# Clearing the block diagonal earlier, and GpSimd's local attention on 256 columns

## The chip, the cores and the metric

The kernel runs on one core of a Trainium2 chip. The core's engines run side by side, each through its own instruction list in order: TensorE (PE in the profile, PEld for its weight loads), VectorE (DVE), ScalarE (ACT), GpSimd (POOL) and SyncE (SP, which issues most DMAs). GpSimd issues some DMAs as well. The metric is device time in microseconds (us) of one execution.

## The reference

Two attention blocks read the same x (2048 tokens, 512 columns, 32 heads of 16) and are mixed by a gate of one number a token:

```python
x = A_x
g = _sigmoid((x * gate_w).sum(-1, keepdims=True))
a = _A_ref(x, A_wqkv, A_wo)   # full softmax attention, 32 heads of 16
b = _B_ref(x, B_wqkv, B_wo)   # each token attends to 8 keys: pos - 0, 2, 4, ... 14
return g * a + (1 - g) * b
```

```python
# _B_ref, the local dilated attention
off = jnp.arange(W) * dil                      # W, dil = 8, 2
idx = pos[:, None] - off[None, :]
logits = jnp.einsum("bhsd,bhswd->bhsw", q, kg) * scale     # kg, vg: k, v at idx
logits = jnp.where(mask[None, None, :, :], logits, -1e9)
attn = _softmax(logits, axis=-1)
o = jnp.einsum("bhsw,bhswd->bhsd", attn, vg)
```

## The kernel before

**Block A** is the bulk. It runs through 32 periods, one for each chunk of 512 queries (4) and group of four heads (8). In a period, PE forms scores of 128 keys by 512 queries for a head (32 x 128 weights from `kt_all`, `qt` streaming) into PSUM tiles (`ring`), ACT takes the exponential of two or three such tiles at a time into `pT`, and PE multiplies `pT` by the values (`vp_all`) into an accumulator. For 3 to 12 tiles a period, the exponential is made on DVE instead (`d_set`, line 1294): a TENSOR_SCALAR from PSUM writes a uint16 number whose bits are a rough exponential, and two more TENSOR_SCALARs within SBUF (`raise1` and `raise2`, lines 1336 and 1339, on 1536 and 3072 columns of `pd_a` or `wall`) add constants to it, so that four weighted copies (`vd_all`) can be summed by PE. These two are called shifts below.

**Block B** is laid beside it. Per chunk of queries and per 8 heads, `scores_of` projects keys into `kt_b` and queries into `qb`; SP copies `qb` head by head into a block-diagonal tile `q_bd` (line 983), which must be zero elsewhere; PE multiplies blocks of the two, DVE copies the result to `sev`, and it goes through DRAM so that each query has its 8 logits in a row. `b_tile` (line 1050) then handles 128 tokens: softmax of `lg` (DVE, GpSimd, ACT), eight products of gathered value rows with attention weights on GpSimd (`av_mul`, line 1109: four into `av`, four into two tiles `prod`), sums of the halves, and a last sum `av_last` (line 1151) into `obb`, which PE transposes (`fin`, line 1190). For 14 of the 16 tiles the sums before the last are DMAs that GpSimd issues and that accumulate into `av` (`av_sum`); for the last two tiles they are GpSimd additions (`av_add`). `HB` (line 923) is the number of columns that one GpSimd product or addition works on; it is `D`, 512.

**The start.** x and the weights of A are loaded; PE transposes x; `k3` (line 619) and `q2` (line 626) rearrange key and query weights for PE's tiles, in part on DVE and in part on GpSimd. `o_q2` (line 635) holds the two halves of q2: group 0 on DVE, group 1 on GpSimd. `init_bd` (line 606) clears `kt_b` and `q_bd`; the first key projections of block B on DVE (`ke`) and the SP copies into `q_bd` wait for it.

**What sets the order.** Every step is an `Op` with an engine, a planned length, a due time and dependencies. `list_schedule` (line 182) simulates the engines with these lengths and always takes the ready step that is due first; `rel` holds a step back in the plan until a time. The result is one order for all, and `chain_on` (line 351) makes each engine keep it. The plan's times don't exist at run time: an engine runs its list as soon as semaphores allow. `GP` (line 111) gives the planned length of a GpSimd step: 0.14 us plus a part proportional to the columns, in which the plan lets no SBUF-to-SBUF work of DVE run (`port`). Calls go through a wrapper, so L371 stands for all instructions of DVE, ACT, GpSimd and SP, and L380 for matmuls.

Of the kernel before, what the change touches and what calls it, by code (L numbers as in the profile page):

```python
# [31 lines left out]
DH = 16  # L32
NG = 8
W = 8
# [14 lines left out]
ROWB = 2 * NGR * QW  # L49
SPREAD = (0.75, 0.88, 0.6)  # L50
STEP = 32.0
ZB = 27.0
WEIGHTS = (0.83984375, 0.70703125, 0.59375)


def _ap(base, dims):
    return bass.AP(tensor=base.tensor, offset=base.offset, ap=[list(d) for d in dims])
# [53 lines left out]
GP = lambda kind, n: [(False, PRE), (True, NS[kind] * n)]  # L111
# [197 lines left out]
def kernel(  # L309
# [15 lines left out]
    S, D = x2d.shape  # L325
# [3 lines left out]
    DC = D // 128  # L329
# [46 lines left out]
    G = Chained(nc.gpsimd, "pool")  # L376
# [20 lines left out]
    def op(eng, occ, fn, dl, **kw):  # L397
        if any(tk.kind == "misc" for tk in kw.get("use", ())):
            dl -= URG[eng]
        o = Op(eng, occ, fn, dl, **kw)  # L400
        ops.append(o)
        return o
# [3 lines left out]
    def tok(tag, cap):  # L406
        name = "banks" if tag in ("misc", "acc") else tag
        if name not in res:
            res[name] = Banks(3) if name == "banks" else Res(cap)
        return Tok(res[name], tag)  # L410
# [15 lines left out]
    for pi in range(NP):  # L426
        first_unit.append(nu)
        n = n_dve[pi]
# [14 lines left out]
    for pi, (own, groups) in enumerate(seq):  # L443
        n = sum(len(g) for g in groups)
# [26 lines left out]
    w0 = DC * 2 * D  # L471
# [39 lines left out]
    q_bd = const.tile([128, 8, QW], BF16, name="q_bd")  # L511
    kt_b = const.tile([128, 2, 2, W - 1 + QW // 2 + 9], BF16, name="kt_b")
# [40 lines left out]
    o_init_p = op("pool", 2.8, init_pool2, -8.0, deps=[o_perm])  # L553
# [49 lines left out]
    o_wq = op("sp", 0.5, load_w(0), -8.5, lat=12.5)  # L603
    o_wv = op("sp", 0.5, load_w(2), -8.4, lat=13.0)
    o_bw = op("sp", 1.0, load_bw, -8.3, lat=19.0)
    def init_bd(n):
        def s():
            if n == 0:
                G.memset(kt_b[:], 0.0)
            G.memset(q_bd[:, 2 * n:2 * n + 2], 0.0)  # L610
        return s
    o_zb = o_init_p
    for n in range(4):
        o_zb = op("pool", 1.0 + 0.5 * (n == 0), init_bd(n), 27.0 + n, deps=[o_zb], rel=ZB)
    o_zr = op("sp", 0.6, load_zero, -8.2, deps=[o_wz], use=[zt], lat=19.0)
    o_wo = op("sp", 5.5, load_wo, WO, rel=WO, lat=10.0)

# [1 line left out]
    def k3(E, i0, i1):  # L619
        def s():  # L620
            wk = wkw.rearrange("p c (i j d) -> p c i j d", i=NG, j=4)
            for e, j in ((0, 3), (1, 0)):
                E.tensor_copy(out=wk3[:, :, i0:i1, e, :], in_=wk[:, :, i0:i1, j, :])
        return s

    def q2(E, i):
        def s():
            a0 = wq[:, :, 4 * i * DH:4 * (i + 1) * DH]
            for e in range(2):
                E.tensor_copy(out=wq2[:, :, 4 * i:4 * i + 4, e, :], in_=a0.rearrange("p c (j d) -> p c j d", j=4))  # L630
        return s

    o_k3 = [op("dve", 0.2, k3(V, 0, 1), -4.0, deps=[o_wk])]
    o_k3 += [op("pool", 2.0, k3(G, 1, NG), -3.0, deps=[o_wk, o_init_p])] * (NG - 1)
    o_q2 = [op("dve", 0.5, q2(V, 0), 0.0, deps=[o_wq]), op("pool", 1.5, q2(G, 1), 5.0, deps=[o_wq, o_k3[1]])]

    def warm():
# [6 lines left out]
    for sc in range(NC):  # L644
        st = {}
# [253 lines left out]
    for sc in range(NC):  # L899
        a = op("pe", 0.9, zmm(sc), GT + sc, full=1, deps=[o_bw, a] + o_xt[sc], alloc=[tzp] if sc == 0 else [],  # L900
               use=[tzp] if sc else [], rel=20.0)
# [18 lines left out]
    o_kvd, o_obt = [], []  # L920
    obt_tiles, obt_tok = {}, {}
    WP = WH // 2
    HB = D
    o_lgw = {}

    def v_rows(t):
# [123 lines left out]
    def b_tile(t):  # L1050

        st = {}
        tb = BT[t]
        cb, e, hb = t // TPC, t // 2 % 2, t % 2
        tvs = [tok("gat", NGA), tok("gat", NGA)]
        tlg, tbb = tok("lg", 2), tok("obb", 1)
# [49 lines left out]

        hn = HB // DH

        def av_mul(hf, wp, w_, c0):
            def s():  # L1110
                if hf == 0:
                    o_ = av[:, wp + w_, c0:c0 + HB]
                else:
                    if w_ == 0 and c0 == 0:
                        st["av", wp] = work.tile([128, WP, D], FP32, name="prod", tag="prod", bufs=NPR)
                    o_ = st["av", wp][:, w_, c0:c0 + HB]
                attn = st["lg"]
                w0 = hf * WH + wp + w_
                a0 = attn[:, 0, w0, 0:1]
                attn_bc = _ap(a0, [list(a0.ap[0]), [8 * W, DC], [1, 8], [0, DH]])  # L1120
                G.tensor_tensor(out=o_.rearrange("p (c h d) -> p c h d", c=DC, d=DH),
                                in0=st["vsh", hf][:, wp + w_, :].rearrange("p (c h d) -> p c h d", c=DC, d=DH),
                                in1=attn_bc, op=ALU.mult)
            return s

# [8 lines left out]
        def av_add(wp, w_, c0):  # L1134
            def s():
                cs = slice(c0, c0 + HB)
                d_, a_ = (wp or 0) + w_, av[:, WP + w_, cs] if wp is None else st["av", wp][:, w_, cs]
                G.tensor_tensor(out=av[:, d_, cs], in0=av[:, d_, cs], in1=a_, op=ALU.add)
            return s

        def sums_of(wp, deps, use):

            if t < NT - 2:
                return op("pool", DMAQ, av_sum(wp), tb + 5, deps=deps, use=use, lat=DMAQ + DMAL, far=True, name=f"B{t}")
            a_ = None
            for w_ in range(WP):
                for c0 in range(0, D, HB):
                    a_ = op("pool", 0.0, av_add(wp, w_, c0), tb + 5, deps=deps, after=[a_], use=use, name=f"B{t}", parts=GP("ff", HB))
            return a_

        def av_last(c0):
            def s():
                if c0 == 0:
                    st["obb"] = work.tile([128, D], BF16, name="obb", tag="obb", bufs=1)
                G.tensor_tensor(out=st["obb"][:, c0:c0 + HB], in0=av[:, 0, c0:c0 + HB], in1=av[:, 1, c0:c0 + HB], op=ALU.add)
            return s
# [14 lines left out]
        tav = tok("av", 1)  # L1171
        b, sums = None, []
        for hf, wp in halves:
            tp_ = tok("prod", NPR) if hf else None
            for n_, (w_, c0) in enumerate((w_, c0) for w_ in range(WP) for c0 in range(0, D, HB)):
# [3 lines left out]
                       name=f"B{t}", parts=GP("bf", HB))  # L1179
# [1 line left out]
                b = sums_of(wp, [b], [tav, tp_])  # L1181
                sums.append(b)
        a1 = sums_of(None, sums, [tav])
        a1 = op("pool", 0.0, av_last(0), tb + 6, deps=[a1], alloc=[tbb], use=[tav], name=f"B{t}", parts=GP("ff", HB))
        a1.lat += SM_LAT[3]
        tk = tok("misc", 2)
        if cb not in obt_tok:
# [16 lines left out]
    for cb in range(NC):  # L1204
        for t in range(TPC * cb, TPC * (cb + 1)):
            v_rows(t)
        for c in range(DC):
            scores_of(cb, c)
        for t in range(TPC * cb, TPC * (cb + 1)):
            b_tile(t)  # L1210
# [157 lines left out]
    for k, us in enumerate(sets):  # L1368
        ring = "rA" if k % 2 == 0 else "rB"
        n = len(us)  # L1370
# [4 lines left out]
        st = dict(k=k, us=us, tn=tn, tp=tp)  # L1375
# [7 lines left out]
        def ex(st=st, n=n, k=k):  # L1383
# [5 lines left out]
               alloc=[tr_], use=[q_tok[pi] for pi in pis], after=[last_qk[0]], scores=k % 2, name=f"qk{k}")  # L1389
# [15 lines left out]
    for pi, (c_, i) in enumerate(periods):  # L1405
        st = {}
# [43 lines left out]
        if i % 2 == 0:  # L1450
# [4 lines left out]
                       use=[to] + ([oat_tok[c_]] if i > 1 else []))  # L1455
# [5 lines left out]
    for t in range(NT):  # L1461
        c_, tt = t // TPC, t % TPC
        st = {}
# [30 lines left out]
        for k0 in range(0, DC + nh, 2):  # L1494
            nk = min(2, DC + nh - k0)
            a = op("pe", WAVE(nk), ab_part(k0), dl - 2.0 + 0.3 * k0, full=nk,
                   deps=[a] if k0 else [o_oat[NG * c_ + ng - 1], o_wo] + o_obt[TPC * c_:TPC * (c_ + 1)],
                   alloc=[tk] if k0 == 0 else [], use=([tk] if k0 else []) + [oat_tok[c_], obt_tok[c_]])
# [67 lines left out]
```

## Time and profile before

| | |
|---|---|
| three runs | 839.07, 845.14, 848.81 us; median 845.14 |
| profiled execution | 837.14 us, span 835.3 us |
| granted TensorE clock in it | 0.991 |
| first exponential of block A starts, last one ends | 23.04 us, 824.4 us |
| GpSimd products `av<-vsh,lg` and `prod<-vsh,lg` | 64 of 1203 ns and 64 of 1250 ns (mean) |
| GpSimd last sums `obb<-av` | 16 of 1447 ns (mean) |
| DVE shifts, `pd_a`: 3072 and 1536 columns | 65 of 1115 ns and 65 of 705 ns (mean) |
| DVE shifts, `wall`: 3072 and 1536 columns | 48 of 1174 ns and 48 of 690 ns (mean) |

How to read the lines: a group has the engine, the operation, tile written <- tiles read, the shape, how many (x); then busy us and the mean in ns of one, then idle time of that engine just before them and what ended it. In a timeline the columns are the start in us from the span's start, the duration, the engine, and in brackets the idle time before and what ended it; where it says x2, neighbours are merged into one line and the duration is that of both. The chain of waits is followed back from the last instruction, and each line of it has a start and a duration. The time of an execution is its span and a little around it (1.84 us here).

### The profile page before, as it was taken

Reading aid. Unit: us, or ns where it says so; the run is one execution under the profiler, and the core shown is the slowest. Engines: PE = TensorE matmul, PEld = TensorE weight load, DVE = VectorE, ACT = ScalarE, POOL = GpSimd, SP = SyncE. Lnnn points to the kernel's source line nnn. Section 1 sums busy time; section 2 is a strip of 40 time slices with the busy share of each in tenths; the row PEclk is TensorE's granted clock in tenths of the full one; section 3 lists DMA queues with packets and bytes.
Section 4 is the critical chain, followed back from the end, with each engine's and each line's share of the span. In section 5 each row is a group of like instructions: output and inputs, shape, how many; then the busy total and the mean of one; then the engine's idle time right before and its main releaser. Section 6 shows DMA issues by size and latency. Waiting matters only on the chain.

```text
span 835.3 us, 18731 instructions
## 1 busy us (share of the span) xinstructions
PE 754.8 (90%) x7426; PEld 249.3 (30%) x7483; DVE 627.8 (75%) x1023; ACT 789.1 (94%) x706; POOL 308.7 (37%) x358
## 2 busy tenths in 40 slices
PE   7999899999989999889889998998999989998996
PEld 4433333333222222222222222222323222222221
DVE  5644866887766779988987777777987687788756
ACT  2899898999999999999999999999999989999994
POOL 5000000545662161654611513434530166394700
PEclk9999999999999999999999999999999989999998
DMA  7301115167447362527362260716153453620000
GB/s 253 78 2 46 42 38 125 39 122 136 122 127 186 51 122 50 131 44 190 76 162 39 68 110 1 155 15 163 32 116 103 78 109 76 121 64 1 1 2 25
DMA packets 118103, 71.44 MB, mean 86 GB/s; under 512 B 76272, under 2 KB 109056, under 8 KB 118016
## 3 DMA queue, kind: packets, MB, share of 16 engines
q1 hardware_dynamic: 111968, 48.23, 22.3%
q0 software_dynamic: 6048, 22.02, 14.6%
q8 instruction: 58, 0.95, 0.5%
q14 instruction: 29, 0.24, 0.1%
HBM read 29.11 MB, written 17.00 MB: 55 GB/s over the span
## 4 chain that ended last, share of the span: by engine, by line
ACT 35%; PE 33%; issue 15%; DVE 11%; DMA 3%; SPq 3%; ACTq 0%; DVEq 0%; POOL 0%
ACT pT L371 35%; PE misc_ps L380 22%; PE ring L380 10%; DVE pd_a L371 4%; DVE wall L371 4%; SPq L371 3%; DMA lg<-lg_scr 1%; DMA xld<-in_A_x_dram 1%; DMA lg_scr<-sev 1%; DMA q_bd<-qb 0%; DMA q_scr<-qa 0%; DVE qb L371 0%; DVE vp_all L371 0%; PE pxt L653 0%; DVE osb L371 0%
## 5 line engine op out<-in xcount | busy, mean ns | idle before, releaser
L371 ACT ACTIVATE pT<-ring 128x1536 bf16<-128x1536 f32 (+1 forms) x684 | 781.2, 1293 | 26.5 <-PE ring L380 17.1
L380 PE MATMUL ring<-qt,kt_all 32*128 32x512 bf16 x1709 | 271.0, 384 | 47.0 <-ACT pT L371 40.1
L380 PE MATMUL misc_ps<-pT,vp_all 128*17 128x512 bf16 (+1 forms) x1709 | 217.1, 385 | 1.2 <-DVE qb L371 0.5
L380 PEld LDWEIGHTS <-kt_all 32*128 32x128 bf16 x2048 | 84.2, 91 | 288.1 <-issue 278.0
L371 DVE TENSOR_SCALAR pd_a<-misc_ps 128x512 uint16<-128x512 f32 x195 | 131.8, 683 | 49.8 <-PE misc_ps L380 46.0
L380 PE MATMUL misc_ps<-qt,kt_all 32*128 32x512 bf16 x339 | 125.7, 382 | 2.6 <-DVE pd_a L371 0.9
L371 DVE TENSOR_SCALAR pd_a<-pd_a 128x1536 uint16<-128x1536 uint16 (+1 forms) x130 | 117.8, 910 | 9.5 <-PE misc_ps L380 8.6
L380 PE MATMUL misc_ps<-z 128*32 128x512 bf16 x374 | 121.9, 388 | 1.6 <-DVE z L371 1.6
L371 DVE TENSOR_SCALAR wall<-misc_ps 128x512 uint16<-128x512 f32 x144 | 96.4, 684 | 25.6 <-PE misc_ps L380 23.4
L371 DVE TENSOR_SCALAR wall<-wall 128x1536 uint16<-128x1536 uint16 x96 | 89.0, 932 | 20.5 <-PE misc_ps L380 19.9
L380 PEld LDWEIGHTS <-vp_all 128*17 128x17 bf16 (+1 forms) x2048 | 59.0, 89 | 84.3 <-issue 66.9
L371 POOL TENSOR_TENSOR prod<-vsh,lg 128x512 f32<-128x512 bf16 x64 | 76.3, 1250 | 0.0
L371 POOL TENSOR_TENSOR av<-vsh,lg 128x512 f32<-128x512 bf16 x64 | 75.4, 1203 | 1.0
L380 PE MATMUL misc_ps<-pd_a,vd_all 128*17 128x512 bf16 x585 | 72.5, 383 | 1.6 <-DVE pd_a L371 1.1
L371 POOL TENSOR_TENSOR rden<-rden,g_rw 128x16 f32<-128x16 f32 x30 | 10.1, 338 | 160.7 <-DVE rden L371 160.6
L380 PE MATMUL misc_ps<-wall,vd_all 128*17 128x512 bf16 x432 | 53.8, 386 | 2.9 <-DVE wall L371 2.8
L380 PEld LDWEIGHTS <-vd_all 128*17 128x17 bf16 x1017 | 31.8, 89 | 60.1 <-issue 53.9
L380 PEld LDWEIGHTS <-z 128*32 128x32 bf16 x374 | 32.6, 96 | 41.4 <-issue 22.1
L380 PE MATMUL misc_ps<-xT,wall 128*32 128x512 bf16 x544 | 41.2, 387 | 3.0 <-DVE wall L371 2.3
L371 POOL TENSOR_SCALAR rr<-rr,omg 128x32 f32<-128x32 f32 x16 | 7.5, 470 | 86.0 <-DVE rr L371 61.6
L371 DVE TENSOR_SCALAR_CACHE_REDUCE kt_all<-misc_ps,rowc 128x512 bf16<-128x512 f32 x32 | 23.9, 749 | 19.7 <-PE misc_ps L380 19.3
L371 POOL TENSOR_TENSOR lg<-lg,mx 128x256 f32<-128x256 f32 x16 | 13.1, 816 | 69.2 <-DVE mx L371 69.2
(95 smaller groups left out, 645.3 us busy)
## 6 DMA issues: line engine op xcount, KB each, us to landing
vsh<-kv_scr SPq DMA_DIRECT2D x128, 128.0 KB
av<-prod POOLq DMA_DIRECT2D x28, 512.0 KB, 5.3
lg_scr<-sev SPq DMA_DIRECT2D x16, 540.0 KB
av<-av POOLq DMA_DIRECT2D x14, 512.0 KB, 5.4
qt<-q_scr SPq DMA_DIRECT2D x30, 128.0 KB
q_bd<-qb SPq DMA_DIRECT2D x128, 16.0 KB
kv_scr<-kvs SPq DMA_DIRECT2D x16, 128.0 KB
lg<-lg_scr SPq DMA_DIRECT2D x64, 32.0 KB
```

The lines of the kernel that those rows point to most:

```text
L371: return chain_on(key, f(*a, **k))
L380: return chain(nc.tensor.matmul(out, lhsT=lhsT, rhs=rhs, start=start, stop=stop, **kw))
```

## The change

The clears lose their release time (`ZB`, 27 in plan time) and their due times of 27 to 30; they follow GpSimd's key-weight copies (`o_k3[1]`) and are due at -2.0 to -1.7, ahead of GpSimd's query-weight copies, due at 5. `HB` becomes 256, so each product, each `av_add` and each last sum becomes two instructions of half the columns, with half-width access patterns of the weights and the value rows.

```diff
-ZB = 27.0
...
-    o_zb = o_init_p
-    for n in range(4):
-        o_zb = op("pool", 1.0 + 0.5 * (n == 0), init_bd(n), 27.0 + n, deps=[o_zb], rel=ZB)
...
     o_k3 = [op("dve", 0.2, k3(V, 0, 1), -4.0, deps=[o_wk])]
     o_k3 += [op("pool", 2.0, k3(G, 1, NG), -3.0, deps=[o_wk, o_init_p])] * (NG - 1)
     def init_bd(n):
         def s():
             if n == 0:
                 G.memset(kt_b[:], 0.0)
             G.memset(q_bd[:, 2 * n:2 * n + 2], 0.0)
         return s
+    o_zb = o_k3[1]
     for n in range(4):
+        o_zb = op("pool", 1.0 + 0.5 * (n == 0), init_bd(n), -2.0 + 0.1 * n, deps=[o_zb])
     o_q2 = [op("dve", 0.5, q2(V, 0), 0.0, deps=[o_wq]), op("pool", 1.5, q2(G, 1), 5.0, deps=[o_wq, o_k3[1]])]
...
-    HB = D
+    HB = D // 2
...
                 w0 = hf * WH + wp + w_
-                a0 = attn[:, 0, w0, 0:1]
-                attn_bc = _ap(a0, [list(a0.ap[0]), [8 * W, DC], [1, 8], [0, DH]])
-                G.tensor_tensor(out=o_.rearrange("p (c h d) -> p c h d", c=DC, d=DH),
-                                in0=st["vsh", hf][:, wp + w_, :].rearrange("p (c h d) -> p c h d", c=DC, d=DH),
+                a0 = attn[:, c0 // 128, w0, 0:1]
+                attn_bc = _ap(a0, [list(a0.ap[0]), [8 * W, HB // 128], [1, 8], [0, DH]])
+                G.tensor_tensor(out=o_.rearrange("p (c h d) -> p c h d", c=HB // 128, d=DH),
+                                in0=st["vsh", hf][:, wp + w_, c0:c0 + HB].rearrange("p (c h d) -> p c h d", c=HB // 128, d=DH),
                                 in1=attn_bc, op=ALU.mult)
...
-        a1 = op("pool", 0.0, av_last(0), tb + 6, deps=[a1], alloc=[tbb], use=[tav], name=f"B{t}", parts=GP("ff", HB))
+        for c0 in range(0, D, HB):
+            a1 = op("pool", 0.0, av_last(c0), tb + 6, deps=[a1], alloc=[] if c0 else [tbb], use=[tav] + ([tbb] if c0 else []),
+                    name=f"B{t}", parts=GP("ff", HB))
```

More of the change, by code (lines that the diff above doesn't have):

```diff
@@ L605 @@
     o_bw = op("sp", 1.0, load_bw, -8.3, lat=19.0)
[L606 to L611, printed above, removed]
-    o_zb = o_init_p
-    for n in range(4):
-        o_zb = op("pool", 1.0 + 0.5 * (n == 0), init_bd(n), 27.0 + n, deps=[o_zb], rel=ZB)
     o_zr = op("sp", 0.6, load_zero, -8.2, deps=[o_wz], use=[zt], lat=19.0)
@@ L634, with init_bd, s @@
     o_k3 += [op("pool", 2.0, k3(G, 1, NG), -3.0, deps=[o_wk, o_init_p])] * (NG - 1)
+    def init_bd(n):
+        def s():
+            if n == 0:
+                G.memset(kt_b[:], 0.0)
+            G.memset(q_bd[:, 2 * n:2 * n + 2], 0.0)
+        return s
+    o_zb = o_k3[1]
+    for n in range(4):
+        o_zb = op("pool", 1.0 + 0.5 * (n == 0), init_bd(n), -2.0 + 0.1 * n, deps=[o_zb])
     o_q2 = [op("dve", 0.5, q2(V, 0), 0.0, deps=[o_wq]), op("pool", 1.5, q2(G, 1), 5.0, deps=[o_wq, o_k3[1]])]
```

## The prediction

> **What bounds the kernel now.** I read the page first, then the waits of ACT, the first 26 us of the chain of waits, and the timelines of GpSimd, DVE and ACT at the places those pointed to. The page:
>
> ```profile
> PE 754.8 (90%) x7426; PEld 249.3 (30%) x7483; DVE 627.8 (75%) x1023; ACT 789.1 (94%) x706; POOL 308.7 (37%) x358
> L371 ACT ACTIVATE pT<-ring 128x1536 bf16<-128x1536 f32 (+1 forms) x684 | 781.2, 1293 | 26.5 <-PE ring L380 17.1
> ```
>
> ACT's 684 exponentials are 781.2 us of the span of 835.3. What is not ACT's own work is little: 23.04 us until the first exponential, 26.5 us of idle time before exponentials (8.9 of them already inside those 23), and about 11 us behind the last one, which ends at 824.4. So an edit pays only if it shortens the 23 us of the start, the 17.6 us that remain of the idle time, or the 11 us of the tail. GpSimd at 37% is no bound by its sum.
>
> The start, from the chain of waits, and what GpSimd and DVE do there:
>
> ```profile
> 13.57 0.69 DVE xT L371
> 14.26 3.34 DVE wall L371 x2
> 17.60 0.04 issue
> 17.64 3.58 PE misc_ps L380 x50
> ...
> 23.04 3.71 ACT pT L371 x3
> ```
>
> ```profile
> 6.58 1.07 POOL L371 COPY wall<-wall 128x448 bf16<-128x448 bf16 x2 [1.23 <-DMA wall<-in_A_wqkv_dram]
> 12.18 0.74 POOL L371 COPY wall<-wq 128x256 bf16<-128x256 bf16 x2 [4.54 <-DMA wq<-in_A_wqkv_dram]
> 12.87 1.01 POOL L371 MEMSET kt_b<- 128x1088 bf16 x1
> 13.81 3.64 POOL L371 MEMSET q_bd<- 128x1024 bf16 x4
> ```
>
> ```profile
> 14.18 3.41 DVE L371 COPY wall<-wq 128x256 bf16<-128x256 bf16 x2
> ```
>
> DVE's two copies of the first query weights (q2, into a part of `wall`) take 3.41 us, and they end at 17.59, just behind GpSimd's memsets (17.45). A copy of 512 columns within SBUF that meets no GpSimd work (the four fills of kt_all at 22.13 and 23.39) takes 0.41, so the rest is waiting for GpSimd. PE's first query projection, and with it the first exponential, stands behind these copies. And between 7.65 and 12.18 GpSimd is idle.
>
> The later idle time shows the same meeting. The worst place, DVE, GpSimd and ACT:
>
> ```profile
> 678.82 3.71 DVE L371 TENSOR_SCALAR wall<-wall 128x3072 uint16<-128x3072 uint16 x1 [1.33 <-PE misc_ps L380]
> ```
>
> ```profile
> 678.70 0.90 POOL L371 DMA_DIRECT2D av<-prod  x1 [0.30 <-POOL prod L371]
> 679.37 2.34 POOL L371 TENSOR_TENSOR prod<-vsh,lg 128x512 f32<-128x512 bf16 x2
> ```
>
> ```profile
> 684.04 2.37 ACT L371 ACTIVATE pT<-ring 128x1536 bf16<-128x1536 f32 x2 [1.02 <-PE ring L380]
> 687.48 3.80 ACT L371 ACTIVATE pT<-ring 128x1536 bf16<-128x1536 f32 x3 [1.07 <-PE misc_ps L380]
> ```
>
> This shift over 3072 columns takes 0.95 where GpSimd is idle (686.07). Here it outlasts a descriptor instruction and two products that stand behind it; ACT then idles 1.02 us, and 1.07 more one step later.
>
> **Part 1, the clears.** The five memsets (1.01 + 3.64, from 12.87 to 17.45 = 4.58 us) move ahead of GpSimd's q2 copies, right behind its key-weight copies. They would run from 7.6 to 12.2, in time that GpSimd now waits for a DMA; its own q2 copies start at 12.2 instead of 12.18. DVE has nothing from SBUF to SBUF in 7.65 to 12.2 (its rows there read PSUM, and such rows keep their 0.69 beside GpSimd work later), so the cover is whole. DVE's q2 copies then start at 14.18 with GpSimd idle. Their price is not in the trace unblocked: at least the 0.29 to 0.35 of the 256-word masks (qa, qt), at most the 0.41 of a 512-column fill, each; I take 0.35, nearest in size, so they end at 14.9 instead of 17.59 (2.7 earlier). What is late next: PE's key projection, until 15.37 instead of waiting to 17.64, which leaves 2.3 us to gain on PE; the two reductions behind it on DVE (17.51 and 18.18) move up 2.6. I take 2.4 us. Bounds: 2.7 above. Below, a loss: if DVE's own key-weight copy at 6.55 were caught by the memsets behind GpSimd's two copies, it would wait to 12.2; DVE's work from there to q2 sums to 4.4 us plus about 1 of PE, so q2 ends at about 18.3, 0.7 later than now. I don't expect it: that copy got its turn between GpSimd's two. The waits for the cleared tiles (DVE's kt_b cast, SP's q_bd stores) come first at about 60 us and hold nothing.
>
> **Part 2, 256 columns.** Costs on GpSimd: 16 columns take 0.22 (rden), 256 take 0.62 (ott), so 0.19 fixed and 1.67 ns a column, which gives 1.05 for 512, the products' own undisturbed time. A split therefore costs 0.19. Split are 128 products, 12 sums of the last two tiles and 16 last sums: 156 x 0.19 = 30 us more on GpSimd, 37% becomes 41%. Of one tile it is 8 + 1 splits, 1.7 us (the last two, with six sums, 2.9). What hides it: a tile's result (obb) is read late. The last obb ends at 787.99 and PE transposes it at 795.4; chunk 0's last user starts at 278. Without that cover it would be 2.9 at the end.
>
> Gains are in DVE's waits. The shifts' means by shape against 0.95 and 0.56 undisturbed: 65 x (1.115 - 0.95) + 48 x (1.174 - 0.95) + 65 x (0.705 - 0.56) + 48 x (0.690 - 0.56) = 37 us of waiting. Met singly, an instruction of 0.62 instead of 1.05 makes the mean wait 41% shorter. But ACT's idle time does not come from the single waits (at most 1.1 us, which the buffers absorb): the gaps that follow a port wait stand before 303.6 (0.53 us), 413.7 (0.66), 684.0 (1.02) and its echo at 687.5 (1.07), 3.3 us together, and each begins in two products whose spans overlap, as above: 2.34 us for two that last 1.3 each. In such a stretch DVE gets no turn between them, and four halves, 4 x 0.62 plus the same overlap, hold it just as long (2.5 to 2.8). So I take 0 for part 2, with bounds of 3.3 gained and 0.5 lost in this execution.
>
> The Trainium skill (SBUF — State Buffer, Who interferes with whom) has the pair of ports go to whoever starts first, for one whole instruction. By that rule the DVE shift of 678.82 would have had its turn after the first product, and with halves 41% of the 3.3 us, 1.4 us, would come back: 833.3 instead of 834.7 below. The trace speaks against it in these stretches (it waited through two) and for it elsewhere.
>
> **Re-planning.** The order of every engine is written out from planned costs, and those of the products change (0.14 + 0.91 planned for one, now twice 0.14 + 0.46). Up to the first product, at 156 us, I expect the order to stay; behind it PE, DVE and ACT instructions may change places. No row prices that; zero is the middle, and it is the widest of the unknowns.
>
> **Sum.** The profiled execution took 837.14 (835.3 span, 1.84 around it): minus 2.4 is 834.7. The three plain runs have a median of 845.14, 8.0 above it, and spread over 9.7 us, so about 1% is what a measurement of this kernel can tell from no change. Minus 2.4 on the median is **842.7**.
>
> **Rivals.**
> *Port waits matter more than this execution shows* (0.33). The plain runs are 8.0 us longer than the profiled one with the same order, so stalls differ from run to run; if they are port meetings, 8.0 + 3.3 = 11.3 us can go. For it: 66 of DVE's shifts and masks from SBUF to SBUF take over 60 ns more than undisturbed, and PE's order stands behind many. Against: ACT lost only 3.3 to them here. With 75% recovered, 845.1 - 2.4 - 8.5 = 834.2; it passes 1% from 6.1 us on.
> *The new order puts PE behind longer stretches* (0.27), slower. Between two accumulating DMAs GpSimd now has four overlapping instructions, and there are 28 such stretches (av<-prod x28). One shift that is caught there and that PE waits for costs ACT 1.02 + 1.07 = 2.1 us. In this execution that is fully so once; seven more make 14.7, less 2.4 gives 857.4. It decides from five or six (10.9 us) on. For it: idle ACT time behind 140 us is only some 9 us of the 17.6, so a different order has more to lose than to win. Against: buffers absorb most meetings.
> *The start's gain does not arrive* (0.04): the caught copy above, 0.7 later, 845.8.
>
> **How the numbers follow.** The forecast has 0.36. Within 1% (836.7 to 853.6): forecast and last rival, 0.40. Faster 0.33, slower 0.27, from the two others. The forecast's own range is 836 to 849: 3.3 + 0.3 better, 0.5 + 3.1 worse by the bounds, and 3 us of re-planning to each side. To leave out no more than 2 in 10 the range reaches past 834.2 and to 857: 832 to 857.
>
> **What would show it.** Memsets at 7.6 to 12.2, DVE's q2 copies under 0.9 us, the first exponential at 20.4 to 20.8; GpSimd near 340 us with products of 0.62; DVE's busy time some 10 us lower. Part 2 is wrong at zero if the 3072-column shifts' worst times fall below 2 us and ACT's idle time behind 140 us falls by more than 3; the slower rival is right if new ACT gaps of 1 us and more stand behind shifts in the stretches between GpSimd's DMAs. The prediction fails if idle time grows where no shift waited: then it is the order.

## The result, and the profile after

| | before | after |
|---|---|---|
| median of 20 runs each, side by side | 843.36 us | 851.56 us |
| ratio after / before | | 1.0091, 95% interval 1.0063 to 1.0119 |
| span of the profiled execution, granted clock | 835.3 us, 0.991 | 844.5 us, 0.986 |
| first exponential | 23.04 us | 18.83 us |
| ACT idle from there to the last exponential | 17.6 us | 31.9 us |

The change makes the kernel 0.9% slower. In the profiled executions the first exponential comes 4.2 us earlier, more than forecast, and 14.3 us of new idle time on ACT take that back and more. These lines of the page of after answer to those of before:

```profile
PE 757.7 (90%) x7440; PEld 252.2 (30%) x7491; DVE 618.0 (73%) x1023; ACT 788.2 (93%) x706; POOL 343.6 (41%) x514
...
L370 ACT ACTIVATE pT<-ring 128x1536 bf16<-128x1536 f32 (+1 forms) x684 | 780.3, 1307 | 36.9 <-PE ring L379 28.6
```

ACT's own work is the same (780.3 us), and its idle time went from 26.5 to 36.9 us though the start holds less of it; 28.6 us of it end with PE's scores in `ring`, 17.1 before. GpSimd's busy time is up by 34.9 us (30 forecast) and DVE's down by 9.8 (10 forecast).

The start, from the timeline of all engines:

```profile
6.16 1.07 POOL L370 COPY wall<-wall 128x448 bf16<-128x448 bf16 x2 [0.81 <-DMA wall<-in_A_wqkv_dram]
7.17 1.00 POOL L370 MEMSET kt_b<- 128x1088 bf16 x1
8.11 3.63 POOL L370 MEMSET q_bd<- 128x1024 bf16 x4
...
13.79 0.35 DVE L370 COPY wall<-wq 128x256 bf16<-128x256 bf16 x2
```

The memsets fill the time in which GpSimd waited for a DMA, and DVE's two query-weight copies take 0.35 us together instead of 3.41. A gap of 1.6 us at 38 us gives part of the 4.2 us back; 2.6 are left from 54 to 91 us. Not all of the 4.2 us come from the clears: e2 below, which has them late, starts its first exponential at 21.84 us, 1.2 earlier than before.

**Where the time went.** I numbered the 684 exponentials, which run in nearly the same order in both kernels, and compared their start times. At number 150 (202 us) after is 2.1 us ahead; from number 178 to 181 it loses 5.7 us, by 210 another 2.8, and the rest in small steps to the end, where it is 9.1 us behind. Up to about 160 us the instruction lists of PE, DVE, ACT and SP are the same in both; behind it all four have another order. The 5.7 us, in the timeline of after:

```profile
224.94 3.45 SPq L370 DMA_DIRECT2D vsh<-kv_scr  x4
...
225.86 2.64 POOL L370 TENSOR_TENSOR prod<-vsh,lg 128x256 f32<-128x256 bf16 x4
225.91 3.42 DVE L370 TENSOR_SCALAR pd_a<-pd_a 128x3072 uint16<-128x3072 uint16 x1
228.49 0.85 SPq L370 DMA_DIRECT2D q_scr<-qa  x1
...
229.25 0.68 DVE L370 TENSOR_SCALAR qb<-misc_ps 128x512 bf16<-128x512 f32 x1
...
232.66 0.32 SPq L370 DMA_DIRECT2D qt<-q_scr  x1
233.07 5.82 SPq L370 DMA_DIRECT2D q_bd<-qb  x8
...
241.56 0.40 PE L379 MATMUL misc_ps<-q_bd,kt_b 128*32 128x128 bf16 x8 [4.99 <-DMA kv_scr<-kvs]
243.43 2.37 ACT L370 ACTIVATE pT<-ring 128x1536 bf16<-128x1536 f32 x2 [5.57 <-PE ring L379]
```

and the same work in before:

```profile
224.73 0.63 SPq L371 DMA_DIRECT2D q_scr<-qa  x1
225.60 0.68 DVE L371 TENSOR_SCALAR qb<-misc_ps 128x512 bf16<-128x512 f32 x1
226.30 6.25 SPq L371 DMA_DIRECT2D q_bd<-qb  x8
...
232.59 1.05 SPq L371 DMA_DIRECT2D qt<-q_scr  x2
...
234.09 0.41 PE L380 MATMUL misc_ps<-q_bd,kt_b 128*32 128x128 bf16 x16 [1.11 <-DVE pd_a L371]
```

Read it from the bottom. ACT idles 5.57 us for PE, and PE idles 4.99 us ahead of the first blocks of block B's sixth unit (a chunk of queries and 8 heads). The releaser that is named, a store, is another user of SP's queue; what PE needs is the eight copies of `qb` into `q_bd`, whose issue ends at 238.89 and the last of which lands at 241.10 by its semaphore. `qb` was ready at 229.93, but SP started the copies only at 233.07, since a load of `qt` stands ahead of them in SP's list. That load reads rows that SP itself had stored at 228.49 to 229.34, and SP stood still for 3.3 us until it could issue it. The view of SP's waits in 229 to 233 us names the landing of that store:

```profile
SPq L370 <- DMA q_scr<-qa: 3.2, 1, 3.2
```

In before the two `qt` loads stand behind the copies. SP waits for such landings in before as well, 37.3 us in 14 waits over the whole run, against 33.1 in 15 in after; what is new is what stands behind the wait. One of SP's lines got a new place, and everything behind it on SP, PE, DVE and ACT waited. The shift of 3.42 us through four products lies in the same place; it delays `qb` by 2.5 us, less than the 3.1 that SP then adds.

**The wait costs twice.** PE's idle time of 4.99 us is followed by a stretch in which its granted clock is halved. The views of 241.1 to 247.9 us in after and of 241 to 248 us in before (stretch and length; busy us of PE, PEld, DVE, ACT and POOL; then the granted clock, the DMA share and GB/s):

```profile
241.10:247.90 6.80, 6.33 (x69) 2.03 (x70) 2.50 (x5) 3.71 (x3) 3.87 (x7) 0.50 0.32 91
```

```profile
241.00:248.00 7.00, 5.59 (x53) 1.58 (x51) 3.22 (x5) 6.89 (x6) 6.15 (x7) 1.00 0.17 51
```

In after the matmuls `misc_ps<-pT,vp_all` take 620 ns there, 382 in before, and ACT is busy for 3.71 of 6.8 us instead of 6.89 of 7.0. In all 14 profiles of this study the clock is either 1 or 0.5. Between start and end it is 0.5 in 69 stretches of 3.4 us or two or three times that. In the 3.4 us ahead of them PE was busy for 0 to 86% (median 59%); in the other stretches of 3.4 us it was busy for 95% (median), though some with as little work are not followed by a low clock. That the idle time brings on the low clock is inferred from this pattern; no run tries it alone. After's gap at 38 us (clock 0.50 from 36.3 to 39.7), the one at 279 us (275.2 to 278.7, behind a wait of 2.40 on PE) and the one at 438 us (435.7 to 439.1, behind a wait of 1.02) lie in such stretches or end with them. Between the first and the last exponential there are 17.1 us of them in after and 6.8 in before.

**Run to run.** Within each kernel the time goes with the granted TensorE clock: fitted over 203 runs of this study (each kernel about its own mean), 5.4 us for every 0.01 of clock, which leaves a spread (one standard deviation) of 1.3 us out of 2.9. (Six more runs, over 1.5% longer than the fastest of the same kernel, are left out here and in the ratios.) So I also give each kernel's mean at clock 0.985 by that slope; with 6 to 18 runs such a mean is good to 0.6 to 1.0 us (95%, an estimate from the 1.3). Before has 842.2 by it (841.8 to 842.5 in three sets of runs; the clocks of the 20 runs in the table above are not on record), after 848.9. So 6.7 us of the difference stand at equal clock, and 1.5 us go with a lower clock in after's runs. Since the clock falls behind PE's waits, a part of these 1.5 us may be the change's too, and of the two figures, 8.2 and 6.7 us, the second is the cautious one.

### The profile page after: what moved, and what is told of

It reads as the page before. It is cut to its first block, busy times and chain, and to the rows that moved or that the text cites. A ratio compares the mean times of both kernels' runs of the same rounds, so it can differ in the third digit from the quotient of the medians.

```text
span 844.5 us, 18903 instructions
## 1 busy us (share of the span) xinstructions
PE 757.7 (90%) x7440; PEld 252.2 (30%) x7491; DVE 618.0 (73%) x1023; ACT 788.2 (93%) x706; POOL 343.6 (41%) x514
## 4 chain that ended last, share of the span: by engine, by line
ACT 42%; PE 23%; issue 18%; DVE 9%; SPq 4%; DMA 4%; DVEq 0%; ACTq 0%
ACT pT L370 42%; PE misc_ps L379 16%; PE ring L379 7%; SPq L370 4%; DVE pd_a L370 3%; DVE wall L370 2%; DMA q_bd<-qb 1%; DMA xld<-in_A_x_dram 1%; ACT lg L370 1%; DMA kv_scr<-kvs 1%; DMA lg<-lg_scr 0%; DMA lg_scr<-sev 0%; DVE qb L370 0%; DVE ssum L370 0%; DMA q_scr<-qa 0%
## 5 line engine op out<-in xcount | busy, mean ns | idle before, releaser
L370 ACT ACTIVATE pT<-ring 128x1536 bf16<-128x1536 f32 (+1 forms) x684 | 780.3, 1307 | 36.9 <-PE ring L379 28.6
L379 PEld LDWEIGHTS <-kt_all 32*128 32x128 bf16 x2048 | 87.1, 91 | 297.3 <-issue 285.6
L379 PE MATMUL misc_ps<-z 128*32 128x512 bf16 x382 | 125.4, 392 | 1.6 <-DVE z L370 1.6
L370 DVE TENSOR_SCALAR wall<-wall 128x1536 uint16<-128x1536 uint16 x96 | 84.0, 878 | 21.7 <-PE misc_ps L379 20.8
L370 POOL TENSOR_TENSOR prod<-vsh,lg 128x256 f32<-128x256 bf16 x128 | 91.1, 794 | 0.0
L370 POOL TENSOR_TENSOR av<-vsh,lg 128x256 f32<-128x256 bf16 x128 | 87.7, 715 | 0.7
L370 POOL TENSOR_TENSOR rden<-rden,g_rw 128x16 f32<-128x16 f32 x30 | 11.7, 390 | 156.6 <-DVE rden L370 156.6
L379 PEld LDWEIGHTS <-z 128*32 128x32 bf16 x382 | 33.8, 97 | 40.5 <-issue 20.6
L379 PE MATMUL misc_ps<-xT,wall 128*32 128x512 bf16 x544 | 39.7, 381 | 1.3 <-DVE vp_all L370 1.1
L370 POOL TENSOR_TENSOR obb<-av 128x256 bf16<-128x256 f32 x32 | 25.4, 806 | 31.0 <-DMA av<-av 26.7
```

Of the source, the lines that this page charges most:

```text
L370: return chain_on(key, f(*a, **k))
L379: return chain(nc.tensor.matmul(out, lhsT=lhsT, rhs=rhs, start=start, stop=stop, **kw))
```

## The experiments

The kernels e1 to e12 ran in three groups (the first four, the next four, the last four), each on another chip and beside runs of before. The last column is one profiled execution each, with a clock of its own (0.975 to 0.991), so differences of a few us in it show nothing.

| label | plan: columns, planned facts | instructions: columns | median us | ratio to before [95%] | mean clock | us at clock 0.985 | ACT idle after the first exponential, profiled |
|---|---|---|---|---|---|---|---|
| before | 512 | 512 | 843.36 | 1 | 0.985 | 842.2 | 17.6 |
| after | 256 | 256 | 851.56 | 1.0091 [1.0063, 1.0119] | 0.981 | 848.9 | 31.9 |
| e1_clears | 512 | 512 | 839.21 | 0.9975 [0.9944, 1.0006] | 0.985 | 839.4 | 20.9 |
| e2_columns | 256, clears late | 256 | 853.35 | 1.0153 [1.0107, 1.0199] | 0.978 | 850.0 | 32.4 |
| e3_order512_instr256 | 512 | 256 | 844.28 | 1.0020 [0.9987, 1.0053] | 0.983 | 843.3 | 25.4 |
| e4_order256_instr512 | 256 | 512 | 855.19 | 1.0161 [1.0116, 1.0205] | 0.981 | 853.2 | 42.5 |
| e5_swap_sp | 256, one load moved | 256 | 847.79 | 1.0055 [1.0019, 1.0091] | 0.984 | 846.6 | 31.7 |
| e6_replan_a | 512, other constant | 512 | 853.73 | 1.0128 [1.0077, 1.0179] | 0.978 | 849.3 | 40.3 |
| e7_replan_b | 512, other constant | 512 | 855.93 | 1.0161 [1.0119, 1.0202] | 0.977 | 851.8 | 41.9 |
| e8_sp_plan | 256, both SP facts | 256 | 839.53 | 0.9973 [0.9950, 0.9997] | 0.990 | 842.5 | 26.2 |
| e9_landing256 | 256, landing | 256 | 846.84 | 1.0047 [1.0017, 1.0077] | 0.980 | 843.7 | 33.1 |
| e10_qbdlen256 | 256, copies' length | 256 | 845.29 | 1.0011 [0.9988, 1.0034] | 0.986 | 844.9 | 31.4 |
| e11_sp_plan512 | 512, both SP facts | 512 | 848.57 | 1.0059 [1.0029, 1.0090] | 0.984 | 848.3 | 33.8 |
| e12_landing512 | 512, landing | 512 | 835.65 | 0.9910 [0.9874, 0.9945] | 0.990 | 838.4 | 21.7 |

Of the kernels made for the experiments, e2 alone has the late clears.

### Each part alone

e1 is after with `HB` back at 512; e2 is after with the clears where before has them.

```diff
-    HB = D // 2
+    HB = D
```

> The early clears alone, products and sums on 512 columns; every engine's list is that of the kernel before, but for the place of the five memsets on GpSimd. In the changed kernel the exponentials around 54 us and 91 us come 2.6 us earlier than before. Theory: this gain is kept to the end, 843.4 - 2.6 = 840.8, ratio 0.997. Rival (the start's gain is given back later whatever the columns): 843.4, ratio 1.000. Rival (the clears themselves set off the loss): over 848, ratio 1.006 or more.

> The 256 columns alone, the clears where they were; every list is that of the changed kernel but for the memsets. The changed kernel loses 844.5 - 835.3 + 2.6 = 11.8 us of span after 150 us. Theory (the two parts add): 843.4 + 11 = 854 to 855, ratio 1.013. Rival (the loss needs the shifted start): 843 to 848, ratio up to 1.005.

Measured: e1 839.21 us, e2 853.35. The clears alone give 2.8 us at equal clock; the loss comes from the other part alone. (In the new order they give 1.1 us, 850.0 in e2 against 848.9 in after; why less was not followed.) That part is two things at once: GpSimd's instructions are shorter, and every engine's order is planned anew. In the traces the lists of e1 are those of before but for the memsets on GpSimd, and those of e2 are those of after but for the same.

### The order and the width, apart

e3 keeps the order of the 512-column plan and issues two halves inside one planned step (the products shown, the sums alike; `HB` is `D` again):

```diff
+    HI = D // 2
...
+                for c1 in range(c0, c0 + HB, HI):
+                    o_ = (st["av", wp][:, w_] if hf else av[:, wp + w_])[:, c1:c1 + HI]
+                    a0 = attn[:, c1 // 128, w0, 0:1]
...
+                                    in1=attn_bc, op=ALU.mult)
```

e4 keeps the order of after: the step of the first half issues the whole 512 columns, that of the second issues nothing (the sums alike):

```diff
+                if c0:
+                    return
+                o_ = st["av", wp][:, w_, :] if hf else av[:, wp + w_, :]
...
+                a0 = attn[:, 0, w0, 0:1]
+                attn_bc = _ap(a0, [list(a0.ap[0]), [8 * W, DC], [1, 8], [0, DH]])
```

> Early clears, GpSimd's products and sums as instructions of 256 columns, but planned as steps of 512, so that PE, DVE, ACT and SP keep the lists of the kernel before to the last instruction. Theory ORDER (the loss is the other order that the plan writes): about as the clears alone, 840 to 842, ratio 0.996 to 0.999. Theory RUN (the halves themselves cost, by 30 us more of GpSimd or by holding up DVE): about as the changed kernel, 850 to 853, ratio 1.008 to 1.012. Half and half: 846.

> Early clears, the order of the changed kernel on PE, DVE, ACT and SP to the last instruction, but each pair of halves issued as one instruction of 512 columns at the first half's place. Theory ORDER: about as the changed kernel, 850 to 853, ratio 1.008 to 1.012. Theory RUN: about as the clears alone, 840 to 842, ratio 0.996 to 0.999.

Measured, with e1 and after as the other two corners, at clock 0.985:

| | instructions of 512 | of 256 | width |
|---|---|---|---|
| order of the 512 plan | e1 839.4 | e3 843.3 | +3.9 |
| order of the 256 plan | e4 853.2 | after 848.9 | -4.3 |
| order | +13.8 | +5.6 | |

The order costs time at either width. The width has no sign of its own: in the new order the halves win, in the old one they lose. So e3 fits neither of its two theories alone. The ACT groups of the pages of e1 and e4, whose GpSimd instructions are the same:

```profile
L370 ACT ACTIVATE pT<-ring 128x1536 bf16<-128x1536 f32 (+1 forms) x684 | 781.5, 1291 | 26.0 <-PE ring L379 17.7
```

```profile
L370 ACT ACTIVATE pT<-ring 128x1536 bf16<-128x1536 f32 (+1 forms) x684 | 782.0, 1295 | 47.6 <-PE ring L379 35.9
```

Idle time before exponentials is 47.6 us in e4 and 26.0 in e1, for the same work. These two executions lie further apart (859.26 and 837.01 us, at clocks of 0.978 and 0.986) than the means do, so the 21.6 us are more than the order's usual cost. Of them 7.9 are one gap, at the place shown above.

How halves can lose in the old order, the timeline of e3 shows at one place:

```profile
476.62 1.22 POOL L370 DMA_DIRECT2D av<-prod  x1 [0.30 <-POOL prod L370]
477.29 2.93 POOL L370 TENSOR_TENSOR prod<-vsh,lg 128x256 f32<-128x256 bf16 x4
477.68 2.70 DVE L370 TENSOR_SCALAR qa<-qs 128x256 uint32<-128x256 uint32 x1
...
481.03 0.37 PE L379 MATMUL misc_ps<-qt,kt_all 32*128 32x512 bf16 x1 [1.98 <-DVE wall L370]
483.06 1.45 ACT L370 ACTIVATE pT<-ring 128x1536 bf16<-128x1536 f32 x1 [2.19 <-PE ring L379]
```

A mask of 256 words is caught behind a descriptor instruction and four products, PE waits 1.98 us for DVE, and ACT idles 2.19. In e1 the stretch of two products there ended at 480.42, and the mask came just behind it, with no gap on ACT:

```profile
480.77 0.28 DVE L370 TENSOR_SCALAR qa<-qs 128x256 uint32<-128x256 uint32 x1
```

Shifts that took over 1.4 us more than undisturbed: 3 in before, 3 in e1, 8 in e3, 5 in after, 3 in e4. All shifts' waiting together is shorter with halves (29.5 us in e3, 35.6 in e1); it is the long waits that became more.

### The place on SP's list

e5 takes the list of after and moves that one `qt` load behind the eight copies.

```diff
+    at = {o.name: n for n, o in enumerate(order)}
+    sp = [o for o in order if o.eng == "sp"]
+    for n, o in enumerate(sp[:-1]):
+        if o.name.startswith("get") and sp[n + 1].name == "diag5":
+            g = order.pop(order.index(o))
+            order.insert(at["diag5"], g)
```

> The changed kernel with one instruction of 18,903 moved: on SP, the load of qt that stands ahead of the eight q_bd copies of the sixth unit (at 232.66 us, where it waits for the stored query rows to land) goes behind them. All other lists are those of the changed kernel. In the changed kernel these copies start 3.1 us after qb is ready (229.9 against 233.07), PE waits 5.0 us for them and ACT idles 5.57. Theory PLACE (the loss sits in q_bd copies that come late for PE): 3 us less, 851.6 - 3 = 848.6, ratio 1.005 to 1.006, and PE's wait there falls to about 2 us. Rival (the delay is absorbed or comes back a few steps on): no change, ratio 1.009.

```profile
232.72 6.71 SPq L370 DMA_DIRECT2D q_bd<-qb  x8
...
239.47 1.58 SPq L370 DMA_DIRECT2D qt<-q_scr  x2
241.72 0.41 PE L379 MATMUL misc_ps<-q_bd,kt_b 128*32 128x128 bf16 x8 [2.38 <-issue]
...
243.59 2.37 ACT L370 ACTIVATE pT<-ring 128x1536 bf16<-128x1536 f32 x2 [2.97 <-PE ring L379]
```

In the timeline of e5 the copies start when `qb` is ready (232.69) instead of 3.1 us later, PE's wait falls from 4.99 to 2.38, ACT's gap from 5.57 to 2.97, and the kernel is 2.3 us faster at equal clock. So the load's place is worth what its wait said, and it is a third of the loss, not the whole. In the profile the run of e5 comes to the place 2.8 us later than after (from 150 to 225 us its clock is 0.95, that of after 1.00) and is 1.1 us ahead seven exponentials on: 3.9 us gained there. Of these 1.3 come behind the gap, where e5's clock is back at 1 from 245.0 us and that of after is at 0.50 until 247.9.

### Is it these 256 columns, or any new order?

e6 and e7 leave the columns at 512 and change one number of the plan, by 1% or less: the fixed part of a GpSimd step from 0.14 to 0.141 us, or the planned time per column of one kind from 1.78 to 1.76 ns. No instruction changes, only the order.

```diff
-PRE = 0.14
+PRE = 0.141
```

```diff
-NS = dict(bb=0.00189, bf=0.00178, ff=0.00212, one=0.0011)
+NS = dict(bb=0.00189, bf=0.00176, ff=0.00212, one=0.0011)
```

> Early clears, everything on 512 columns; the one edit is a planned length, PRE from 0.14 to 0.141 us for GpSimd steps, which changes no instruction but writes another order behind 150 us (some 560 of 879 rows of DVE's list change place). Theory DRAW (any re-plan costs, because the order of before is a good one among many and the plan does not see what makes it good): 846 to 853, ratio 1.004 to 1.012. Theory COLUMNS (it is the longer or split GpSimd steps that spoil the order): as the clears alone, 840 to 842, ratio 0.996 to 0.999.

> As the run before, another planned length: 0.00176 instead of 0.00178 us a column for bf16 products, so GpSimd steps are planned slightly shorter. Theory DRAW: 846 to 853, ratio 1.004 to 1.012. Theory COLUMNS: 840 to 842 or less, ratio 0.999 or lower.

Measured: 9.9 and 12.4 us slower than e1 at equal clock, more than the whole change lost and, as medians, more than theory DRAW allowed. The plan sees nothing of it: its own time for the end of the last exponential is 813.5 us for before, 814.1 for after, 814.3 and 814.6 for e6 and e7. And the place is the same again, in the timeline of e6:

```profile
225.81 0.68 DVE L370 TENSOR_SCALAR qb<-misc_ps 128x512 bf16<-128x512 f32 x1
225.91 0.63 SPq L370 DMA_DIRECT2D q_scr<-qa  x1
...
231.63 0.32 SPq L370 DMA_DIRECT2D qt<-q_scr  x1
232.05 5.99 SPq L370 DMA_DIRECT2D q_bd<-qb  x8
...
241.90 2.37 ACT L370 ACTIVATE pT<-ring 128x1536 bf16<-128x1536 f32 x2 [6.14 <-PE ring L379]
```

`qb` was ready at 226.5, and the copies start at 232.05. No shift is caught here: the list of SP is enough. (SP's waits in 226 to 232 us are 4.9 us for the landing of `q_scr<-qa`.)

### Telling the plan what SP does

The plan lets a load follow a store on SP as soon as the store is issued, and counts 2.0 us for four `q_bd` copies, which take 2.5 to 3.7 (4.94 to 7.49 for the groups of eight in before and e1). e8 tells it both, e9 the landing alone, e10 the length alone (all on after); e11 is both and e12 the landing alone, on e1. The landing, where `far` makes a step on the same engine wait out `lat` too, and the length:

```diff
-        w = [op("sp", 0.5, put(0), dl - 5.0, deps=[c], use=[tqs], lat=2.2), op("sp", 0.5, put(1), dl - 4.0, deps=[b], use=[tqa], lat=2.2)]
+        w = [op("sp", 0.5, put(0), dl - 5.0, deps=[c], use=[tqs], lat=2.2), op("sp", 0.5, put(1), dl - 4.0, deps=[b], use=[tqa], lat=3.2, far=True)]
```

```diff
-            dg.append(op("sp", 2.0, diag(h0), dl - 8 + h0 / 4, deps=[a, o_zb], after=dg[:], alloc=[] if h0 else [tqd], use=[tqe] + ([tqd] if h0 else []), lat=4.2))
+            dg.append(op("sp", 2.9, diag(h0), dl - 8 + h0 / 4, deps=[a, o_zb], after=dg[:], alloc=[] if h0 else [tqd], use=[tqe] + ([tqd] if h0 else []), lat=5.1))
```

> The changed kernel, planned with what the traces show of SP: four q_bd copies take it 2.9 us instead of the 2.0 planned (5.7 to 5.9 for eight), and a load of qt waits until the stored rows have landed (3.2 planned behind the store) instead of being issued at once. Theory BLIND (the loss comes from what the plan does not know of SP's list): the place at 233 us closes, 840 to 845, ratio 0.997 to 1.002. Rival DRAW (one more order, as good or bad as any): 846 to 853, ratio 1.004 to 1.012.

> The changed kernel, planned with one of the two corrections of SP alone: a load of qt waits for the stored rows to land. At 233 us the q_bd copies go ahead of the load, as in the swap by hand; PE's list stays that of the changed kernel over its first two thirds. Theory PLACE: about as the swap, 847 to 849, ratio 1.003 to 1.006. If this one blind spot were the whole loss: 840 to 842, ratio 0.997 to 1.000.

> The changed kernel, planned with the other correction alone: 2.9 us for four q_bd copies. Loads of qt still stand ahead of the sixth unit's copies. Theory PLACE: the gap at 233 us stays, and the list before 150 us changes too, so 848 to 855, ratio 1.006 to 1.014. Theory LENGTH (it is the too short planned q_bd copies that matter): 838 to 842, ratio 0.995 to 1.000.

> Early clears, 512 columns, planned with both corrections; 512 columns otherwise as the clears alone. Theory: with a plan that knows SP the width matters little, so as the same plan with 256 columns (839.5): 836 to 844, ratio 0.993 to 1.002. Rival DRAW (the run with 256 was luck): 846 to 853, ratio 1.004 to 1.012.

> Early clears, 512 columns, planned with the landing alone; the lists are those of the clears alone but for the last third. Theory: as the clears alone or a little better, 837 to 842, ratio 0.994 to 0.999. Rival DRAW (any change of order costs): 844 to 852, ratio 1.002 to 1.011.

Measured, against the kernel that each is made from, at equal clock: e9 -5.2 us, e8 -6.4, e10 -4.0; e12 -1.0, e11 +8.9. In e9 the copies stand ahead of both loads again, and PE's wait at the sixth unit is 1.54 us. Up to 556 us its lists of PE, DVE, ACT and GpSimd are those of after, and only loads of `qt` stand elsewhere on SP. From exponential 178 to 185, where after loses 6.8 us against before, e9 gains 5.5 on after, with the shift of 3.44 us still caught ahead of it. e10 came out otherwise than its theory PLACE said: its order keeps the load ahead of the copies, and yet it gained. The timeline of e10:

```profile
231.20 1.61 SPq L370 DMA_DIRECT2D qt<-q_scr  x2
...
235.46 5.84 SPq L370 DMA_DIRECT2D q_bd<-qb  x8
...
242.86 0.41 PE L379 MATMUL misc_ps<-q_bd,kt_b 128*32 128x128 bf16 x16 [2.13 <-DMA q_bd<-qb]
```

The copies are later than in after (235.46), but PE's list has their user later too, and PE waits 2.13 us instead of 4.99. So the load's place alone does not set the wait; the place of the user in PE's list counts too. e11 came out otherwise as well: with the same two facts the 512-column plan loses, by longer and new gaps on ACT elsewhere. One grew from 3.76 us (e1, at 95 us) to 6.68 (at 98 us; e8 has it too), and one of 3.21 at 190 us is new.

The three plans with truer times on the order of after all gained. For e9 the traces show that the loads' places did it, up to 556 us; for e8 and e10, whose whole order is new, a lucky draw is not excluded, and e11 shows that truer times are no safeguard. e12, whose lists are those of e1 up to about 665 us but for the places of `qt` loads on SP, is the best of all: 0.9% faster than before as measured. Its six runs had a mean clock of 0.990; at equal clock it is 3.8 us (0.5%) ahead of before and 1.0 us ahead of e1, which is no more than the two can be told apart by. Why e11 loses and e12 does not was not followed further. (The plan's own end of the last exponential is 813.5 us for e1 and e12, 819.9 for e11 and 817.5 for e8: it tells e11 from e12, but it has e8, which gained, on the wrong side.)

## Why the prediction was wrong

The forecast was 842.7 from 845.14, 2.4 us down; the kernel became 8.2 us slower by the medians side by side, 6.7 at equal clock. 851.56 lies within the range of 832 to 857, at the end that the slower rival had put there, but it came there in the main for another reason. By its steps:

- **Part 1, the clears: right.** 2.4 us forecast, 2.8 measured (e1). Memsets at 7.2 to 11.7 (7.6 to 12.2 forecast), DVE's copies 0.35 us together (under 0.9; the sum had 0.35 for each), the first exponential at 18.8, 1.6 us earlier than forecast. A gap at 38 us, in a stretch at clock 0.50, takes about as much back; that the two cancel is luck (e3 and e4, with the same clears, have no such gap).
- **Part 2, GpSimd's cost: right.** 34.9 us more against 30. That all of it is hidden is not shown by itself: in the same order (e3) it and DVE's waits together cost 3.9.
- **Part 2, DVE's waits: right in the mechanism, too low in size.** DVE's busy time fell by 9.8 us for the 10 forecast, and in stretches of overlapping products four halves lasted about as long as forecast (2.64 and 2.93 us for 2.5 to 2.8). But the bounds at ACT were 3.3 gained and 0.5 lost; in the same order the width lost 3.9 (e3) and in the new one it gained 4.3. The step took the stretches as fixed meetings, but which shift meets one changes with the timing: in e3 eight shifts were caught for over 1.4 us, in e1 three. The sum also had no term for the clock: the "echo" of 1.07 us at 687.5 lies in a stretch at clock 0.50 (683.5 to 690.3), behind a wait on PE.
- **The Trainium skill's rule** (SBUF — State Buffer, Who interferes with whom), one whole instruction to whoever starts first, was set against the trace there, and the runs decide as the trace of before did. By the rule the shift of 225.91 in after would have had its turn after one product; it waited for the four. The 1.4 us that the rule would have given back did not come in e3; what the halves won in the new order (4.3) was not traced to single waits.
- **Re-planning: this step failed.** "No row prices that; zero is the middle", with "3 us of re-planning to each side", for "PE, DVE and ACT instructions" that change places. Measured, the new order costs 5.6 us with halves and 13.8 with whole products, and two other new orders of the same instructions cost 9.9 and 12.4. The size was wrong by a factor of two to five, and the middle was wrong too: the eight other planned orders (after, e6 to e12, of both widths) stand 6.6 us behind e1 on average, and e12 alone is ahead of it. And the place was missing: the largest single loss comes from SP's list, which the step did not name, through a load of `qt` that got ahead of the `q_bd` copies. That the order stays up to the first products was right (to about 160 us). The argument for it stood in the slower rival's own text, that a new order has more to lose than to win with so little idle time left; it was used for a chance and not for the forecast.
- **The slower rival (857.4): right in sign, in the main wrong in place.** It laid the loss to shifts caught in GpSimd's stretches. Such catches grew from 3 to 5, and two new gaps on ACT do stand behind them (1.82 us at 438.4, 1.12 at 690.0; before has 2.1 us in gaps of this kind and size). But at the largest loss, the gap of 5.57 us, the load's place on SP decides: e9 regains most of it with the shift still caught, and e6 has it with no shift caught. The prediction's own test named this case: idle time that grows where no shift waited is the order.
- **The faster rival (834.2): not borne out.** It took the 8.0 us between the plain runs and the profiled one for port meetings that halves would shorten. In the same order halves lost 3.9 us (e3). The runs' times go with the granted clock, which leaves 1.3 us of spread for all else; whether port meetings set off some of the waits on PE behind which the clock falls is not shown.

**What stays open.** Behind exponential 150 after loses 11.2 us against before. Of the 6.8 us lost from exponential 178 to 185, e5 gives 3.9 back and e9 5.5 by the loads' places; the caught shift that delays `qb`, and the place of the user in PE's list, share the rest, and were not measured singly. The two gaps at 276 and 279 us (1.54 and 1.53) stand behind a PE wait of 2.4 ahead of the eighth unit and were not tried alone. The rest lies in smaller steps that I did not follow.

## What to carry to other kernels

Where a kernel's order is written out from planned costs, an edit that touches a planned cost is two edits, and the second one, the new order, can be worth more than the first: here up to 13.8 us against 2.8 to 4.3. Issue the new instructions in the old order first (as e3 does), then re-plan, and take several orders before judging the edit. In this profile, with an engine at 94%, a new order had little idle time to win and much to lose (seven of eight were slower than e1), so its cost is to be forecast above zero. A wait on PE is to be priced with the low clock behind it. And before a spread between runs is given to a mechanism, it should be set against the granted clock.

## What the hardware did that I had not expected

- GpSimd instructions that follow each other closely keep DVE's SBUF-to-SBUF work out together, not singly: 3.42 us for a shift of 0.95 behind four products, 2.70 for a mask of 0.28 to 0.35. Cutting them in two shortened the sum of the shifts' waits (35.6 to 29.5 us, e1 to e3) and made the long ones more frequent (3 to 8).
- A load on SP behind the store that it reads stood still for 3.3 us (after) and 5.1 us (e6) behind the store's issue, for its landing, and held eight copies that had nothing to do with either.
- The granted clock is halved for 3.4 us, or two or three times that, often behind a wait of only 1 to 2.4 us on PE (2.40 us ahead of 275.2 in after, 1.02 ahead of 435.7). By the run, the time goes with the mean clock by 5.4 us for 0.01 over all kernels (4.1 to 9.7 within each), on a single core.
